# Requeueing three ScalarE operations in the first key groups: one exponential behind the next group's first fork copy, one behind its copy s7, one V copy behind the copy of a fifth product

## The chip, the cores and the metric

The kernel runs on one core of one Trainium2 chip. The metric is the device time of an execution in microseconds (us); 0.1% of it is 0.72 us. Engines: PE is TensorE, DVE is VectorE, ACT is ScalarE, POOL is GpSimd.

## The reference, cut to what matters

```python
x = A_x                                             # [1, 2048, 1024] bf16
q, k, v = split(layernorm(x) @ wqkv)                # 32 heads of 32
phi = lambda t: where(t > 0, t + 1, exp(t)) + 1e-6
kv = einsum("bhsd,bhse->bhde", phi(k), v)           # sums over all tokens
...                                                 # attention output, then a gated MLP
```

Only the beginning matters here: the layer norm, the k and v projections and the running sum `kv`.

## The kernel before

Tokens come in 16 tiles of 128. V of tiles 0 to 3 is computed by plain products ("V pieces"). Everything else is computed for pairs of tiles in groups of seven products instead of eight (a Strassen-like scheme on sums of input blocks). `k0` is the k projection of tiles 0 and 1, both halves of its columns; `v2` is V of tiles 4 and 5, and so on. Groups run in the order k0, v2, k1, v3, k2, v4. A PSUM bank is the buffer in which the matmuls of one product are summed. `hook(i)` runs what was left in `pend[i]` before, mostly by the previous group, then what the main part registered for that place. One group is:

```python
def sgroup(...):
    prod(a, X(0, 0), W(0, 0), True, "P1")                 # four matmuls into PSUM bank a
    ident_act(bank(b), bank(a), ..., name + "fk1")        # first fork: ACT copies bank a to bank b
    hook(1)
    prod(f, SX(2), TW(2), True, "P7")
    ident_act(s7, bank(f), ...)                           # copy s7
    hook(2)
    prod(b, SX(1), TW(1), False, "P6")                    # needs the first fork
    ident_act(bank(c), bank(b), ..., name + "fk2")        # second fork
    hook(3)
    prod(a, X(1, 0), W(1, 0), False, "P2")
    for f_ in e11(bank(a), B_bank[a]): f_()               # k group: exp on ACT, two DVE ops (phi)
    hook(4)
    prod(c, SX(0), TW(0), False, "P5")                    # needs the second fork
    ident_act(sc, bank(c), ...)                           # copy sc
    s22 = e22(bank(f), ..., sc, bc); s22[0]()             # DVE addition
    hook(5)
    prod(b, X(1, 1), TW(3), False, "P4")
    s21 = e21(bank(b), ..., s7, b7); s21[0]()             # DVE addition
    hook(6)                                               # v2: 64 small matmuls, the KV sum of tiles 0 and 1
    for f_ in s22[1:2]: f_()                              # exp of s22, on ACT
    prod(c, SX(3), W(1, 1), False, "P3")                  # overwrites what sc reads: waits for sc
    s12 = list(e12(bank(c), B_bank[c]))
    if isphi: s12.pop(0)()                                # exp of s12, on ACT
    ...
    pend[1] = list(s22[2:]) + s12 + list(s21[1:])         # run at hook(1) of the next group
    hook(7)
```

`SX` and `TW` are sums and differences of input and weight blocks, which DVE makes; I call them all sums. A phi step is the pair of DVE operations on lines 854 and 857 that follows an exponential. TensorE runs the products in this order; counted so, P7 is the second, P6 the third, P5 the fifth and P3 the last. Each engine takes its own operations in the order in which they are recorded.

Of the kernel before, what the change touches and what calls it, by code (L numbers as in the profile page):

```python
# [132 lines left out]
def bass_sequential_preLN__linear_attn_block__glu_gated_reglu__prompt_kernel(  # L133
# [71 lines left out]
    with es:  # L205
# [148 lines left out]
        def bank(b, w=512):  # L354
            return ps[:, b, 0:w]
# [184 lines left out]
        def alloc_bank(pool, copied=False):  # L540

            b = min((b for b in pool if not (copied and b in partial)), key=lambda b: bank_last[b])
            if not copied:
                partial.discard(b)
            touch_bank(b)
            return b
# [219 lines left out]
        def mm(out_ap, lhsT, rhs, start, stop, reads, bbuf, name, skip=False):  # L766
            return PL.add(
                "pe",
                lambda e: e.matmul(out_ap, lhsT, rhs, start=start, stop=stop, skip_group_check=skip),  # L769
                reads=reads, writes=[bbuf], name=name,  # L770
            )

        def ident_act(dst, src, reads, writes, name, func=ACTF.Identity):
            PL.add("act", lambda e: e.activation(out=dst, in_=src, func=func), reads=reads, writes=writes, name=name)  # L774
# [70 lines left out]
        def phi_steps(src, src_buf, dst_ap, dst_buf, name):  # L845
            k = phi_ctr[0] % NPH
            phi_ctr[0] += 1

            def ex():
                PL.add("act", lambda e: e.activation(out=Et[:, k, :], in_=src, func=ACTF.Exp),  # L850
                       reads=[src_buf], writes=[B_E[k]], name=name + "_exp")

            def fin():
                PL.add("dve", lambda e: e.tensor_scalar(out=Et[:, k, :], in0=Et[:, k, :], scalar1=1.0,  # L854
                                                      scalar2=1e-6, op0=ALU.min, op1=ALU.add),
                       reads=[], writes=[B_E[k]], name=name + "_e2")
                PL.add("dve", lambda e: e.scalar_tensor_tensor(out=dst_ap, in0=src, scalar=C1, in1=Et[:, k, :],  # L857
                                                               op0=ALU.add, op1=ALU.max),
                       reads=[src_buf, B_E[k]], writes=[dst_buf], name=name + "_phi")
            return ex, fin  # L860
# [84 lines left out]
        def xnT_buf(st, dc):  # L945
            return B_xnT[st][0 if dc < HDC else 1]
# [3 lines left out]
                b = banks[i % len(banks)]  # L950
                mm(bank(b, 512), zeros_t[:, 0:P], zeros_t, True, True, [B_zeros], B_bank[b], "dummy")

        def v_piece(st, h, mid=()):
            b = alloc_bank(P1_POOL)
            nt = ND2 + h
            mid = dict(mid)
            for dc in range(NDC):
                if dc in mid:
                    mid[dc]()
                if st < 2:  # L960
                    xa, bx = xcT[:, st, dc, :], B_xcT[st][dc // HDC]
                else:
                    xa, bx = xnT[:, dc, st * P:(st + 1) * P], xnT_buf(st, dc)
                mm(bank(b, NW), xa, wkv[:, dc, nt * NW:(nt + 1) * NW],
                   dc == 0, dc == NDC - 1, [bx, B_wkv[nt][0 if dc < WKH else 1]], B_bank[b],
                   "v_%d_%d" % (st, h))
            v_copy(b, st, h)

        v_k = {}

        def v_out(st, j):
            n0 = (st % NV) * H + j * GPN * HPG
            return vh[:, n0:n0 + GPN * HPG, 0:Dh]

        def gw(ap):
            return ap.rearrange("p (n w) -> p n w", w=Dh)

        def v_copy(b, st, j):
            sc, rd = (1.0, []) if st >= 2 else (rstd[:, v_k[st], :], [B_rstd[v_k[st]]])
            PL.add("act", lambda e: e.activation(out=v_out(st, j), in_=gw(bank(b)), func=ACTF.Identity, scale=sc),  # L980
                   reads=[B_bank[b]] + rd, writes=[B_v[st % NV][j]], name="v_%d_%d" % (st, j))
# [42 lines left out]
            add(1, s(0), xb(0, 0), ALU.subtract, [B_Sx[0][p]] + bx(0, 0))  # L1024
            add(3, xb(1, 0), s(1), ALU.subtract, [B_Sx[1][p]] + bx(1, 0))

        def sgroup(pool, tok_major, X, SX, W, TW, e11, e12, e21, e22, name, hooks=(), isphi=True, last=False):

            hooks = dict(hooks)

            def prod(b, x, w, start, nm):
                (xf, xr), (wf, wr) = x, w
                for kk in range(KH):
                    xa, wa = xf(kk), wf(kk)
                    l, r = (xa, wa) if tok_major else (wa, xa)
                    o = bank(b)
                    if len(r.shape) == 3:
                        o = o.rearrange("p (a b) -> p a b", b=r.shape[2])
                    mm(o, l, r, start and kk == 0, kk == KH - 1, xr + wr, B_bank[b], name + nm, skip=True)

            def hook(i):
                for f_ in pend.pop(i, ()):
                    f_()
                if i in hooks:
                    hooks[i]()

            a = alloc_bank(pool)
            f = alloc_bank(pool)
            b = alloc_bank(pool, True)
            prod(a, X(0, 0), W(0, 0), True, "P1")  # L1050
            ident_act(bank(b), bank(a), [B_bank[a]], [B_bank[b]], name + "fk1")
            hook(1)
            prod(f, SX(2), TW(2), True, "P7")
            grp[0] += 1
            s7, b7 = [(atmp, B_at), (btmp[:, 1, :], B_bt[1])][grp[0] % 2]
            sc, bc = btmp[:, 0, :], B_bt[0]
            ident_act(s7, bank(f), [B_bank[f]], [b7], name + "s7")
            hook(2)
            c = alloc_bank(pool, True)
            prod(b, SX(1), TW(1), False, "P6")  # L1060
            ident_act(bank(c), bank(b), [B_bank[b]], [B_bank[c]], name + "fk2")
            hook(3)
            prod(a, X(1, 0), W(1, 0), False, "P2")
            for f_ in e11(bank(a), B_bank[a]):
                f_()
            hook(4)
            prod(c, SX(0), TW(0), False, "P5")
            ident_act(sc, bank(c), [B_bank[c]], [bc], name + "sc")
            s22 = e22(bank(f), B_bank[f], sc, bc)
            s22[0]()  # L1070
            hook(5)
            prod(b, X(1, 1), TW(3), False, "P4")
            s21 = e21(bank(b), B_bank[b], s7, b7)
            s21[0]()
            hook(6)
            for f_ in s22[1:2]:
                f_()
            prod(c, SX(3), W(1, 1), False, "P3")
            s12 = list(e12(bank(c), B_bank[c]))
            if isphi:  # L1080
                s12.pop(0)()
            if last:
                pend[1] = s12 + [s21[1]]
                return [s22[2], s21[2]]
            pend[1] = list(s22[2:]) + s12 + list(s21[1:])
            hook(7)

        pend = {}
# [8 lines left out]
        def add_phi(dst, dst_buf, name):  # L1097
            def go(p_, pb, s_, sb_):
                def add():
                    PL.add("dve", lambda e: e.tensor_tensor(out=s_, in0=p_, in1=s_, op=ALU.add), reads=[pb],  # L1100
                           writes=[sb_], name=name + "_add")
                return (add,) + phi_steps(s_, sb_, dst, dst_buf, name)
            return go

        def x_ops(p):
            def X(k, t):
                st = 2 * p + t
                return (lambda kk: xnT[:, k * KH + kk, st * P:(st + 1) * P]), [B_xnT[st][k]]

            def SX(i):  # L1110
                return (lambda kk: Sx(i)[:, kk, p * P:(p + 1) * P]), [B_Sx[i][p]]
            return X, SX
# [26 lines left out]
        def k_group(p, hooks=()):  # L1139
            X, SX = x_ops(p)  # L1140
            W, TW = w_ops(wkv, bw_k, tw_k, B_TWk)

            def dst(t, h):
                st = 2 * p + t
                return pk_ap(st)[:, h * NW:(h + 1) * NW], B_pk[pk_slot(st)][h]

            def pl(t, h):
                d, db = dst(t, h)
                return lambda b, bb: phi_steps(b, bb, d, db, "k_%d_%d" % (2 * p + t, h))
            sgroup(P1_POOL, True, X, SX, W, TW, pl(0, 0), pl(0, 1),  # L1150
                   add_phi(*dst(1, 0), "k_%d_0" % (2 * p + 1)),
                   add_phi(*dst(1, 1), "k_%d_1" % (2 * p + 1)), "k%d" % p, hooks)

        def v_group(p, hooks=()):
            X, SX = x_ops(p)
# [844 lines left out]
        twk.pop(0)()  # L2000
        twv.pop(0)()
        twv.pop(0)()
        v_piece(3, 1)
        for i in range(2):
            load_wq(i)
        NP_ = NST // 2
# [50 lines left out]
        for p in range(NP_):  # L2057
            nq = NQ.get(p, (0, 0))
            hooks, sq = kv_hooks(p, nq)
# [5 lines left out]
            if p + 2 < NP_:  # L2065
                late = []
# [37 lines left out]
        for r in range(2):  # L2104
            for ct in range(NG // 2):
                hooks = {}
# [41 lines left out]
        for p_ in range(NPASS):  # L2148
            fill = []
            for q in range(NPAIR):  # L2150
# [5 lines left out]
                mid = [[], [], [], [], []]  # L2156
# [59 lines left out]
            late = []  # L2216
            if p_ + 1 < NPASS:
                late = [(lambda t=t: early_c(t), (0, t)) for t in range(STB)]
# [81 lines left out]
```

## Time and profile before

| | before |
|---|---|
| time, median of the first 3 runs | 722.19 us (722.02 to 722.98) |
| span of the profile | 720.5 us |
| PE, DVE, ACT busy | 99%, 82%, 50% |
| PE idle in 24 to 36 us | 1.07 us |

The prediction shows the rows of the profile. Two more lines of its timeline (start and duration in us, engine, line, operation) serve as marks from here on: the DVE sum after which DVE never rests until its last phi step in v2, and the first product of k1.

```profile
24.39 1.22 DVE L991 TENSOR_TENSOR RC<-RAB,RC 128x2048 f16<-128x2048 bf16 x1
36.88 1.03 PE L769 MATMUL ps<-RAB 128*128 128x512 bf16 x4
```

I call the start of that sum T. Here T is 24.39, and the first product of k1 starts at T + 12.49.

### The profile page before, as it was taken

How to read it: one execution, taken by the hardware profiler on the slowest of the kernel's cores; microseconds unless marked ns; L12 is line 12 of the kernel's file. 1: busy time of each engine (PE TensorE's matmuls, PEld its weight loads, DVE VectorE, ACT ScalarE, POOL GpSimd, SP SyncE). 2: the span in 40 equal slices, each digit the busy share in tenths (PEclk: the TensorE clock that was granted, in tenths of full speed). 3: DMA queues.
4: the chain of work that ended last, by engine and by line, in shares of the span. 5: the costliest groups of instructions: out<-in, count | busy, mean ns of one | idle time of the engine just before them, and what ended most of it. 6: DMA issues, size and time to landing. Idle time of an engine off the chain costs nothing.

```text
span 720.5 us, 12877 instructions
## 1 busy us (share of the span) xinstructions
PE 714.3 (99%) x4901; PEld 380.0 (53%) x4901; DVE 588.9 (82%) x1030; ACT 358.9 (50%) x626; POOL 110.8 (15%) x178
## 2 busy tenths in 40 slices
PE   8999999999999999999999999999999999999998
PEld 3344444444444444444444568865555555447887
DVE  6988867899776889888988787887889877888885
ACT  4977666764842466677756111035455445423010
POOL 3321100000350103332321001310000000000331
PEclk9999999999999999999999999999999999999999
DMA  9852344015998797999998999994554572037997
GB/s 295 260 113 65 38 136 157 9 30 97 216 202 264 222 284 236 276 320 297 296 281 266 313 251 317 318 215 119 145 169 139 160 245 84 1 95 248 322 323 183
DMA packets 195101, 144.17 MB, mean 200 GB/s; under 512 B 53984, under 2 KB 172512, under 8 KB 195040
## 3 DMA queue, kind: packets, MB, share of 16 engines
q1 hardware_dynamic: 190048, 138.77, 65.9%
q0 software_dynamic: 4032, 3.67, 3.6%
q10 hardware_dynamic: 960, 0.92, 0.4%
q8 instruction: 38, 0.62, 0.4%
q14 instruction: 23, 0.19, 0.1%
HBM read 98.76 MB, written 32.51 MB: 182 GB/s over the span
## 4 chain that ended last, share of the span: by engine, by line
PE 95%; DVE 2%; DMA 1%; ACT 1%; issue 1%; SPq 0%; ACTq 0%
PE ps L769 95%; DMA RAB<-in_A_wqkv_dram 1%; DVE RWG L1016 0%; DVE RE L857 0%; DVE RX L1100 0%; DVE RE L1674 0%; DVE RX L854 0%; DVE RH L1016 0%; ACT RXH L809 0%; DVE RC L991 0%; DVE RW L991 0%; ACT ps L774 0%; PE ps L910 0%; DVE RWG L1614 0%; SPq L567 0%
## 5 line engine op out<-in xcount | busy, mean ns | idle before, releaser
L774 ACT ACTIVATE ps<-ps 128x512 f32<-128x512 f32 (+1 forms) x193 | 108.9, 565 | 220.8 <-PE ps L769 212.1
L769 PE MATMUL ps<-RC,RO 128*128 128x512 f16 x616 | 143.0, 369 | 0.0
L769 PE MATMUL ps<-RH,RWG 128*128 128x512 bf16 x448 | 108.1, 379 | 0.0
L769 PEld LDWEIGHTS ps<-RC,RO 128*128 128x128 f16 x616 | 60.3, 98 | 63.5
L769 PE MATMUL ps<-RC,RWG 128*128 128x512 f16 x320 | 76.9, 379 | 0.3 <-ACT ps L774 0.2
L769 PEld LDWEIGHTS ps<-RH,RWG 128*128 128x128 bf16 x448 | 43.8, 98 | 46.9
L1483 DVE TENSOR_TENSOR RAB<-ps,RAB 128x512 bf16<-128x512 f32 x56 | 37.3, 686 | 31.3 <-PE ps L769 31.3
L769 PE MATMUL ps<-RH,RO 128*128 128x512 bf16 (+1 forms) x256 | 61.2, 379 | 0.0
L1683 POOL DMA_DIRECT2D out_dram<-RX x20 | 17.9, 1281 | 263.7 <-DVE RX L1674 221.5
L769 PE MATMUL ps<-RW,RE 128*128 128x512 bf16 x256 | 57.6, 380 | 0.0
L769 PE MATMUL ps<-RW,RAB 128*128 128x256 f16 (+3 forms) x362 | 52.9, 301 | 0.0
L769 PEld LDWEIGHTS ps<-RC,RWG 128*128 128x128 bf16 (+1 forms) x320 | 30.0, 98 | 40.3 <-ACT ps L774 6.3
L774 ACT ACTIVATE RE<-ps 128x512 f32<-128x512 f32 (+1 forms) x64 | 31.5, 503 | 37.8 <-PE ps L769 37.8
L769 PE MATMUL ps<-RAB 128*128 128x512 bf16 (+2 forms) x238 | 49.8, 348 | 0.0
L769 PEld LDWEIGHTS ps<-RW,RAB 128*128 128x128 f16 (+1 forms) x362 | 35.3, 98 | 14.5
L1674 DVE TENSOR_TENSOR RE<-ps,RE 128x512 f32<-128x512 f32 x44 | 30.2, 686 | 14.2 <-PE ps L769 13.7
L774 ACT ACTIVATE RAB<-ps 128x512 bf16<-128x512 f32 x56 | 33.3, 595 | 16.7 <-PE ps L769 16.4
L1367 DVE TENSOR_TENSOR RO<-RWG 128x1024 f16<-128x1024 bf16 x54 | 36.9, 684 | 4.5 <-DMA RWG<-in_B_W_up_dram 4.5
L769 PEld LDWEIGHTS ps<-RH,RO 128*128 128x128 f16 (+1 forms) x256 | 24.4, 98 | 29.9 <-ACT RX L774 1.5
L1478 ACT ACTIVATE RAB<-RAB 128x1024 bf16<-128x1024 bf16 x28 | 29.5, 1055 | 19.3 <-DVE RAB L1469 18.7
L1469 DVE TENSOR_TENSOR RAB<-ps,RE 128x512 bf16<-128x512 f32 x56 | 37.1, 685 | 2.1 <-PE ps L769 1.7
L769 PEld LDWEIGHTS ps<-RW,RE 128*128 128x128 bf16 x256 | 24.0, 98 | 27.9 <-DVE RXH L1265 0.4
(170 smaller groups left out, 1170.3 us busy)
## 6 DMA issues: line engine op xcount, KB each, us to landing
RWG<-in_B_W_gate_dram SPq DMA_DIRECT2D x28, 512.0 KB, 6.2
RWG<-in_B_W_up_dram SPq DMA_DIRECT2D x28, 512.0 KB, 5.2
RW<-l_scr SPq DMA_DIRECT2D x20, 448.0 KB, 5.6
RW<-in_B_W_down_dram SPq DMA_DIRECT2D x14, 512.0 KB, 5.4
t_scr<-RW SPq DMA_DIRECT2D x14, 512.0 KB, 4.8
l_scr<-RX SPq DMA_DIRECT2D x7, 1024.0 KB, 6.1
RE<-l_scr SPq DMA_DIRECT2D x15, 448.0 KB, 4.9
RE<-in_A_x_dram SPq DMA_DIRECT2D x23, 256.0 KB, 3.7
```

What stands on the lines that cost most here:

```text
L769: lambda e: e.matmul(out_ap, lhsT, rhs, start=start, stop=stop, skip_group_check=skip),
L774: PL.add("act", lambda e: e.activation(out=dst, in_=src, func=func), reads=reads, writes=writes, name=name)
L1367: PL.add(eng, lambda e: e.tensor_tensor(out=tb(j, u), in0=f0(u), in1=f1(u), op=ALU.subtract), reads=[B_w[i + x] for x in r] + ([B_T[k + x] ...
L1469: PL.add("dve", lambda e: e.tensor_tensor(out=d, in0=src, in1=ftmp[:, u, :], op=ALU.add), reads=[bsrc, B_s5[u]], writes=[db], name=name)
L1478: PL.add("act", lambda e: e.activation(out=d, in_=d, func=ACTF.Relu), reads=[], writes=db, name=name)
L1483: PL.add("dve", lambda e: e.tensor_tensor(out=d, in0=bank(b), in1=d, op=ALU.mult), reads=[B_bank[b]], writes=[db], name=name)
L1674: PL.add(eng, lambda e: e.tensor_tensor(out=dst, in0=in0, in1=in1, op=op), reads=reads, writes=writes, name=name)
L1683: PL.add("pool", lambda e: e.dma_start(dst, src, accum_op=ALU.add), reads=[bsrc], writes=[B_hscr[st]], slot=sl, name="acc_%d_%d" % (st, dh))
```

## The change

The intent is to let the fork copies, on which TensorE waits, run earlier on ACT, by queueing operations behind them that nobody needs soon.

```diff
-        def v_piece(st, h, mid=()):
+        def v_piece(st, h, mid=(), late=False):
 ...
-            v_copy(b, st, h)
+            if late:
+                pend[5] = [lambda: v_copy(b, st, h)]      # behind sc of the next group, k0
+            else:
+                v_copy(b, st, h)
 ... in sgroup:
-            if isphi:
+            if isphi and not lazy:
                 s12.pop(0)()
 ...
-            pend[1] = list(s22[2:]) + s12 + list(s21[1:])
+            if lazy:
+                pend[1] = s12[:1] + list(s22[2:]) + s12[1:]   # exp of s12 behind the first fork
+                pend[2] = list(s21[1:])                       # exp of s21 behind s7
+            else:
+                pend[1] = list(s22[2:]) + s12 + list(s21[1:])
 ... in k_group: lazy=p < 2          # k0 and k1, so the forks of v2 and v3
 ... in the main part:
-        v_piece(3, 1)
+        v_piece(3, 1, late=True)
```

Only the ACT queue changes its order; the other four queues are the same.

More of the change, by code (lines that the diff above doesn't have):

```diff
@@ L1025, in x_sums, with sgroup @@
             add(3, xb(1, 0), s(1), ALU.subtract, [B_Sx[1][p]] + bx(1, 0))
-        def sgroup(pool, tok_major, X, SX, W, TW, e11, e12, e21, e22, name, hooks=(), isphi=True, last=False):
+        def sgroup(pool, tok_major, X, SX, W, TW, e11, e12, e21, e22, name, hooks=(), isphi=True, last=False, lazy=False):
             hooks = dict(hooks)
@@ L1151, in k_group @@
                    add_phi(*dst(1, 0), "k_%d_0" % (2 * p + 1)),
-                   add_phi(*dst(1, 1), "k_%d_1" % (2 * p + 1)), "k%d" % p, hooks)
+                   add_phi(*dst(1, 1), "k_%d_1" % (2 * p + 1)), "k%d" % p, hooks, lazy=p < 2)
         def v_group(p, hooks=()):
```

## The prediction

> **What bounds the kernel now.** First the page: its busy row, to see which engine is full.
>
> ```profile
> PE 714.3 (99%) x4901; PEld 380.0 (53%) x4901; DVE 588.9 (82%) x1030; ACT 358.9 (50%) x626; POOL 110.8 (15%) x178
> ```
>
> TensorE (PE) is busy in 714.3 us of a span of 720.5 us, and the clock row of the page shows it at 0.9 or more in every slice. Nothing that only reorders ScalarE (ACT) can therefore gain more than the few microseconds in which PE stands still. The change touches the stretch from the end of the direct V pieces to the second V group, some 23 to 50 us, so I took busy time by stretch next (columns: stretch, its length, then PE, weight load, DVE, ACT, POOL busy).
>
> ```profile
> 24.00:36.00 12.00, 10.93 (x110) 4.47 (x109) 11.76 (x20) 10.78 (x24) 3.11 (x7) 1.00 0.81 254
> 36.00:45.00 9.00, 8.94 (x52) 3.58 (x40) 8.52 (x21) 6.80 (x16) 2.82 (x7) 1.00 0.54 119
> 45.00:51.00 6.00, 5.96 (x89) 2.84 (x90) 5.66 (x13) 4.34 (x9) 0.00 (x0) 1.00 0.27 53
> ```
>
> In 24 to 36 us PE is idle for 12.00 - 10.93 = 1.07 us; in the next two stretches for 0.06 and 0.04 us. So what can be won lies in the first stretch, and there VectorE (DVE) is fuller than PE: 11.76 of 12.00 us. Third, the timeline of that stretch, PE alone (start, duration):
>
> ```profile
> 23.31 1.03 PE L769 MATMUL ps<-RC,RWG 128*128 128x512 f16 x4
> 24.54 1.04 PE L769 MATMUL ps<-RC,RWG 128*128 128x512 f16 x4 [0.20 <-ACT ps L774]
> ...
> 29.73 1.03 PE L769 MATMUL ps<-RW,RWG 128*128 128x512 f16 x4
> 31.56 1.04 PE L769 MATMUL ps<-RW,RWG 128*128 128x512 f16 x4 [0.81 <-ACT ps L774]
> ```
>
> These are products of four matmuls. In a run without waits they start 0.865 us apart (27.14, 28.00, 28.86, 29.73). From 23.31 to 24.54 is 1.23 us, so 0.36 us is lost at the first fork copy of group k0; from 29.73 to 31.56 is 1.83 us, so 0.96 us is lost at that of v2. Both wait for the fork copy on ACT (line 774, the tile ps to ps), and these are the waits that the change aims at.
>
> Last, what stands after them, from the same timeline for DVE and PE:
>
> ```profile
> 34.02 0.69 DVE L857 SCALAR_TENSOR_TENSOR RE<-ps,RX 128x512 bf16<-128x512 f32 x1
> 34.62 0.28 DVE L854 TENSOR_SCALAR RX<-RX 128x512 bf16<-128x512 bf16 x1
> 34.94 0.69 DVE L857 SCALAR_TENSOR_TENSOR RE<-RX 128x512 bf16<-128x512 f32 x1
> 35.24 0.83 PE L769 MATMUL ps<-RE 128*32 128x33 bf16 x64
> 36.00 1.04 PE L769 MATMUL ps<-RAB,RH 128*128 128x512 bf16 x4
> ```
>
> The 64 small matmuls add tokens 0 and 1 to the KV sum. The quarter for tile 1's first half needs the DVE operation that runs from 34.94 to 35.63; the chain of waits shows PE starting again at 35.69, and 32 matmuls later, at 36.00, the last product of v2 follows. So PE already waits there for DVE. How long has DVE been late? In the timeline its only idle time is 0.46 us before 23.93, for a rstd from POOL. From 23.93 to 35.63 every start follows the one before at the pitch the operation has elsewhere (1.14 us for a 128x2048 sum, 0.60 for an addition, 0.32 then 0.61 for the two halves of phi). **DVE, not ACT, sets the time at which PE leaves this stretch.**
>
> **What the Trainium skill says.** "PSUM — Partial Sum Buffer", section Engine vs sequencer instructions: the queues of ScalarE and VectorE are strict FIFO. That is the whole lever of this change (a fork copy ready early still waits behind what is queued ahead), and the trace agrees: the copy at 30.91 follows two exponentials at 29.90 and 30.44 though its product began at 28.86. "ScalarE: Activation LUTs", section What ACT_TABLE_LOAD costs: an activation runs at one element per cycle for every function, and back-to-back ones overlap by about 93 ns. The trace agrees roughly: exponential and copy take 0.58 to 0.63 us and start 0.47 to 0.54 us apart, so swapping them costs nothing by itself. "Perfetto Trace Analysis", section Tensor Engine Instruction: the end of a matmul in the profile is an estimate. I therefore reckon with starts only. No page bears on how long an ACT wait for PE takes; I take it from the trace.
>
> **The change part by part.** Nothing is added or removed. Comparing the programs' order, PE, DVE, POOL and SP are identical; only ACT has three moves.
>
> Two measures first. Where ACT sits idle, a fork copy starts 1.12 to 1.13 us after its product starts (36.88 to 38.00; 56.28 to 57.41), and PE's next product starts 0.63 to 0.66 us after the copy starts (38.00 to 38.63; 30.91 to 31.56).
>
> 1. V copy of tile 3 (0.58 us at 23.41), moved behind the copy "sc" of k0. k0's first product began about 23.31 - 0.87 = 22.44, so the fork can start at 22.44 + 1.13 = 23.57 instead of 23.89 and the next product at 24.22 instead of 24.54: 0.32 us earlier. Some is lost again inside k0: the second fork is ready at 25.35, the fifth product at 26.00, sc at 27.13, and the last product waits for sc (27.13 + 0.66 = 27.79). v2 then begins at 28.65 instead of 28.86: 0.21 us earlier. The V copy now runs at about 27.6, then the 1.05 us statistic, ending near 29.25. ACT has idled 0.93 us before 29.90 for a DVE addition, so both fit and the exponential at 29.90 stays.
>
> 2. v2: the fork goes before one exponential. It cannot pass the exponential at 29.90, which was queued earlier, so it starts at about 30.42 instead of 30.91, and the third product at 31.07 instead of 31.56 (0.49 us). The exponentials then follow at 30.92 and 31.88; the second fork is at 32.41 instead of 32.77, the fifth product at 33.06 instead of 33.41. PE would reach the small matmuls at about 34.89 instead of 35.24, **0.35 us earlier, and stop at the quarter that DVE delivers at 35.63.** DVE's order is unchanged and all its inputs come before it needs them (exponentials ending about 31.5 and 32.5 for operations at 33.70 and 34.62). So PE resumes at 35.69 as before: 0.00 us gained.
>
> 3. v3: at 43.05 its first product starts; the fork is ready at 44.18 and ran at 44.39. Now it runs at 44.18 and the third product starts at 44.83 instead of 45.04. But the queue up to the second fork holds the same five activations, and the fork now makes ACT idle from 43.92 to 44.18: copies and exponentials at 44.68, 45.15, 45.64, second fork at 46.16 instead of 46.11. The fifth product starts at 46.16 + 0.65 = 46.81 instead of 46.77. So 0.21 us is won and given back two products later: 0.04 us lost.
>
> Sum: 0.00 + 0.04 us on 722.19 us, that is, no change that a timing can see: 722.2 us.
>
> **The rivals.**
>
> The chain of waits is right and ACT is the bound. It shows the V copy and the fork as pieces of the path:
>
> ```profile
> 23.50 0.49 ACT RE L980
> 23.99 0.50 ACT ps L774
> ...
> 27.34 0.61 ACT RX L774
> 27.94 0.28 DVE RX L854
> ```
>
> If the steps from ACT to DVE are real, part 1 brings DVE forward. Against it: the DVE operation at 27.92 comes 1.14 us after the sum at 26.78, its ordinary pitch, and its input (the exponential at 26.71) was done at 27.30; the view attributes the step to the last signal. If I am wrong here, the gain is up to the 1.07 us of idle PE time in 24 to 36 us: 721.1 us.
>
> A new wait. The late V copy holds its PSUM bank some 4 us longer; the program shows v2's first fork copy now writes into that bank and waits for ACT itself as well as PE. By the above the copy ends near 28.2, before the fork at 30.4. Also, should the statistic for tile 7 slip, its normalisation at 38.20 could. It has a second of two halves running after 34.37 anyway, so the slip is not on that path. If one of these did bind: 0.3 to 0.6 us lost, 722.5 to 722.8 us.
>
> DVE itself shifts. POOL gates DVE at 23.93 and takes its numbers from ACT at 20.82 to 22.0, before the first move. So no gain and no loss from there.
>
> **Range and chances.** I give about 75% to no visible change, 17% to a gain of 0.3 to 1.1 us and 8% to a loss of that kind. Three runs of the kernel before lie between 722.02 and 722.98, so a median may move by half a microsecond by itself. Range: 721.3 to 723.0 us. A change of 2% would be 14 us, thirteen times the idle time of PE in the stretch that the change can reach: faster 0.4%, same 99.2%, slower 0.4%.
>
> **What would show it.** Right, if the idle time before the third products of k0 and v2 falls (0.20 to about 0, 0.81 to about 0.5), if a wait of PE for DVE line 857 appears or grows to about 0.4 us just before 35.69, if v2's last product still starts at 36.00 and DVE is without idle time from 23.93 to 35.63; and if in v3 the fifth product starts within 0.1 us of 46.77. Wrong, if v2's last product starts clearly before 35.9, which would mean that DVE did follow ACT; or if DVE shows idle time there, waiting for an exponential that moved.

## The result, and the profile after

| | before | after |
|---|---|---|
| median | 722.35 us (722.02 to 722.98, 4 runs) | 722.80 us (722.38 to 723.14, 4 runs) |
| span of the profile | 720.5 us | 720.8 us |
| T | 24.39 | 24.72 |
| first product of k1 | T + 12.49 | T + 12.48 |

The ratio is 1.0005, 95% interval 0.9988 to 1.0022: the same. (The ratio is not the ratio of the medians, which is 1.0006 here.)

The queue of ACT at the first fork of v2, before and then after: two exponentials stood ahead of the fork copy, now one does.

```profile
29.90 0.63 ACT L850 ACTIVATE RX<-RX 128x512 bf16<-128x512 f32 x1 [0.93 <-DVE RX L1100]
30.44 0.58 ACT L850 ACTIVATE RX<-ps 128x512 bf16<-128x512 f32 x1
30.91 0.59 ACT L774 ACTIVATE ps<-ps 128x512 f32<-128x512 f32 x1
```

```profile
30.23 0.63 ACT L850 ACTIVATE RX<-RX 128x512 bf16<-128x512 f32 x1 [0.83 <-DVE RX L1107]
30.76 0.58 ACT L774 ACTIVATE ps<-ps 128x512 f32<-128x512 f32 x1
31.28 0.58 ACT L850 ACTIVATE RX<-ps 128x512 bf16<-128x512 f32 x1
```

The timeline after: two DVE lines, the mark T and the last phi step of v2, then the PE lines from the second product of k0 on.

```profile
24.72 1.22 DVE L994 TENSOR_TENSOR RC<-RAB,RC 128x2048 f16<-128x2048 bf16 x1
35.27 0.69 DVE L857 SCALAR_TENSOR_TENSOR RE<-RX 128x512 bf16<-128x512 f32 x1
```

```profile
23.20 1.03 PE L769 MATMUL ps<-RC,RWG 128*128 128x512 f16 x4
24.49 1.02 PE L769 MATMUL ps<-RC,RWG 128*128 128x512 f16 x4 [0.26 <-DVE RC L994]
...
31.40 1.04 PE L769 MATMUL ps<-RW,RWG 128*128 128x512 f16 x4 [0.71 <-ACT ps L774]
...
33.40 1.04 PE L769 MATMUL ps<-RW,RWG 128*128 128x512 f16 x4
34.27 1.03 PE L769 MATMUL ps<-RW,RAB 128*128 128x512 f16 x4
35.23 0.38 PE L769 MATMUL ps<-RE 128*32 128x33 bf16 x32
36.02 0.38 PE L769 MATMUL ps<-RE 128*32 128x33 bf16 x32 [0.40 <-DVE RE L857]
...
37.20 1.03 PE L769 MATMUL ps<-RAB 128*128 128x512 bf16 x4
```

Read them against T, not against the clock, because T itself moved by 0.33 us. The third product of v2 started at T + 7.17 before (31.56) and at T + 6.68 after: 0.49 us earlier. The small matmuls began at T + 10.85 and now at T + 10.51: 0.34 us earlier. Then the second half of them waits for DVE, and it starts at T + 11.30 in both kernels (35.69 and 36.02). DVE's last phi step starts at T + 10.55 in both (34.94 and 35.27). The gain has become the wait of 0.40 us on line 857, and k1 starts at the same T + 12.48 or 12.49. In the kernel before, DVE was the last by little: from the start of the small matmuls to k1 it is 1.64 us there, 1.97 us after, and 1.51 us in `dve_minus` below, where nothing waits. So DVE cost PE 0.13 us before and 0.46 us after.

### The profile page after: what moved, and what is told of

The parts are those of the page before. It is cut to its first block, busy times and chain, and to the rows that moved or that the text cites. A ratio compares the mean times of both kernels' runs of the same rounds, so it can differ in the third digit from the quotient of the medians.

```text
span 720.8 us, 12822 instructions
## 1 busy us (share of the span) xinstructions
PE 710.7 (99%) x4846; PEld 380.4 (53%) x4901; DVE 588.9 (82%) x1030; ACT 358.8 (50%) x626; POOL 110.0 (15%) x178
## 4 chain that ended last, share of the span: by engine, by line
PE 94%; DMA 2%; DVE 1%; issue 1%; ACT 1%; SPq 0%; ACTq 0%
PE ps L769 94%; DMA RE<-in_A_x_dram 1%; DMA RAB<-in_A_wqkv_dram 1%; SPq L567 0%; ACT ps L774 0%; DVE RC L994 0%; ACT RX L850 0%; DVE RE L857 0%; DVE RE L1681 0%; DVE st L783 0%; DVE RW L994 0%; ACT RXH L774 0%; DVE RWG L1621 0%; ACT RXH L809 0%; DVE RX L854 0%
## 5 line engine op out<-in xcount | busy, mean ns | idle before, releaser
L769 PE MATMUL ps<-RH,RO 128*128 128x512 bf16 (+1 forms) x228 | 55.2, 379 | 1.5
```

Source lines behind the costliest of these rows:

```text
L769: lambda e: e.matmul(out_ap, lhsT, rhs, start=start, stop=stop, skip_group_check=skip),
```

## The experiments

All experiments were read by T, because a whole execution varies by more than the change can do. "k1" is the start of k1's first product. The last phi step of v2 starts at T + 10.55 or 10.56 in the first six rows.

| run | T | k1 after T | span | span - T |
|---|---|---|---|---|
| before | 24.39 | 12.49 | 720.5 | 696.1 |
| before_again | 25.00 | 12.49 | 721.1 | 696.1 |
| after | 24.72 | 12.48 | 720.8 | 696.1 |
| after_again | 24.50 | 12.49 | 720.6 | 696.1 |
| v_only | 24.27 | 12.49 | 720.4 | 696.1 |
| lazy_only | 24.44 | 12.48 | 720.5 | 696.1 |
| act_plus | 24.44 | 12.69 | 720.7 | 696.3 |
| dve_plus | 25.07 | 15.00 | 723.6 | 698.5 |
| dve_minus | 24.97 | 12.02 | 720.5 | 695.5 |
| kv_late_before | 24.69 | 12.11 | 720.8 | 696.1 |
| kv_late_after | 24.64 | 11.78 | 720.4 | 695.8 |
| best | 24.26 | 11.10 | 721.0 | 696.7 |
| best2 | 24.21 | 11.12 | 720.1 | 695.9 |

In the last four rows the small matmuls that stood in front of k1, half or all of them, come behind its first product, so the third column is not comparable there and the last one is.

**The same two programs again.** No edit.

> The changed kernel once more, unaltered. Theory (VectorE sets when TensorE leaves v2): ratio to the kernel before within 0.9990 to 1.0010, no sign settled. In its trace the gap between the start of v2's seventh product and its third-listed product stays near 1.73 us (1.83 in the kernel before), and the last product of v2 starts 0.3 to 0.4 us after the end of the last phi step on VectorE, wherever that lies. If VectorE's chain starts as early as in the kernel before (its 128x2048 sum at 24.39 rather than 24.72), the product starts near 36.0 again. Rival (the change itself makes VectorE late by 0.33 us): the chain starts at about 24.7 again, and in no trace of the kernel before.

> The kernel before against itself: what a ratio shows where nothing differs. Ratio 0.9990 to 1.0010. Its trace is the second one of this program: if the start of VectorE's chain moves between 24.3 and 24.8 us without any change of the program, the 0.33 us by which the changed kernel's profile is later is no effect of the change; if it lies at 24.39 again, that reading loses ground.

Measured: after_again 722.31 us, ratio 1.0002 (0.9988 to 1.0015); before_again, the kernel before against itself, 722.60 us, ratio 1.0003 (0.9991 to 1.0016). Nothing separates the change from no change. In after_again the v2 pitch was 1.66 us (expected near 1.73), the rest as expected. The trace of before_again settles where the 0.33 us came from; its DVE lines:

```profile
21.81 1.23 DVE L991 TENSOR_TENSOR RC<-RAB 128x2048 f16<-128x2048 bf16 x1 [1.04 <-DMA RAB<-in_A_wqkv_dram]
...
25.00 1.22 DVE L991 TENSOR_TENSOR RC<-RAB,RC 128x2048 f16<-128x2048 bf16 x1
```

An unchanged program had T at 25.00, later than the changed one, after DVE had waited 1.04 us for a load of key weights. The same wait (1.13 us) stands in the profile after, and not in the first profile before. So a later T needs no change of the program, and T accounts for the whole difference between the two profiled spans: span less T is 696.1 us in all six rows.

**One part at a time.** `v_only` has `lazy=False`; `lazy_only` has the V copy in its old place.

> Only the V copy is moved; the exponentials stay. Theory: the fork of k0 starts directly behind the 1.05 us statistic, so that the idle time of TensorE before k0's second product that needs it falls from 0.36 us in pitch to under 0.1 us, unless VectorE's sum for that product is late, as in the changed kernel's profile; the fork of v2 still runs behind two exponentials, and the pitch there stays at 1.8 to 1.9 us. The last product of v2 follows the end of VectorE's last phi step by 0.3 to 0.4 us. Rival (chain of waits right): that product comes 0.2 to 0.35 us earlier than in the kernel before with VectorE's chain starting at the same time.

> Only the exponentials are moved; the V copy stays. Theory: in k0 the pitch of 1.23 us stays (the fork behind the V copy); in v2 the pitch falls from 1.83 to 1.3 to 1.75 us, and the time won ends in a wait for VectorE's last phi step of 0.2 to 0.5 us; in v3 the third product comes 0.2 to 0.3 us earlier after the group's start and the fifth within 0.05 us of before (3.72 us after the group's start). The last product of v2 follows the end of VectorE's last phi step by 0.3 to 0.4 us. Rival: the last product of v2 comes about 0.4 us earlier relative to the start of VectorE's chain.

Measured: in `v_only` the loss at k0's fork is gone (second product at 23.19, fourth at 24.92: 1.73 us, two free pitches), the pitch at v2's fork grew to 2.2 us, more than the 1.8 to 1.9 expected because PE arrived earlier at the same fork, and the time is 722.13 us for one run. In `lazy_only` the small matmuls began early and waited 0.40 us for DVE; 722.25 us for one run. Two pitches there missed the forecast: 1.39 us at k0's fork (1.23 expected), and about 1.2 us at v2's (1.3 to 1.75 expected; reckoned back from the fourth product at 32.00, because the view joins the second and the third). Each part does its work on ACT's queue, and in both k1 starts at T + 12.48 or 12.49. The rival, a step from ACT to DVE, would have shown there as 0.2 to 0.4 us less.

In `lazy_only` v3 also behaves as in the changed kernel. PE lines of v3, first, fourth and fifth product, in the kernel before and then in the changed kernel (in `lazy_only` the distances are 2.60 and 3.70 us):

```profile
43.05 1.03 PE L769 MATMUL ps<-RAB 128*128 128x512 bf16 x4
...
45.91 1.03 PE L769 MATMUL ps<-RAB 128*128 128x512 bf16 x4
46.77 1.03 PE L769 MATMUL ps<-RW,RWG 128*128 128x512 f16 x4
```

```profile
43.38 1.03 PE L769 MATMUL ps<-RAB 128*128 128x512 bf16 x4
...
45.97 1.03 PE L769 MATMUL ps<-RAB 128*128 128x512 bf16 x4
47.08 1.04 PE L769 MATMUL ps<-RW,RWG 128*128 128x512 f16 x4
```

From the first product to the fourth it is 2.86 us before and 2.59 after, so the third came 0.27 us earlier; to the fifth it is 3.72 and 3.70. The second fork ends the same queue of five activations either way: from the first of them to the second fork it is 2.71 us before (43.40 to 46.11) and 2.69 after (43.72 to 46.41). What changed is where ACT stands still, ahead of the second fork before and ahead of the first one after. So the gain is given back one wait later.

**More DVE work, more ACT work.** The first edit does one weight sum three times; the second does the exponential of s22 in k0 twice. Both on top of the change, results unchanged.

```diff
         twv.pop(0)()
         twv.pop(0)()
+        again()            # the last of these sums once more
+        again()            # and once more
         v_piece(3, 1, late=True)
```

```diff
-            for f_ in s22[1:2]:
+            for f_ in s22[1:2] * (2 if name == "k0" else 1):
                 f_()
```

> The changed kernel with one VectorE sum of 128x2048 (1.22 us, 1.14 to 1.25 us of pitch) done three times instead of once, results unchanged: 2.3 to 2.5 us more VectorE work ahead of v2. Theory (VectorE is what TensorE follows out of v2): TensorE leaves v2 2.3 to 2.5 us later counted from the start of the VectorE chain, that is, the first product of k1 starts 14.8 to 15.0 us after the sum that starts at 24.72 in the changed kernel, instead of 12.48, and the whole execution is about 2.4 us longer: ratio to the kernel before 1.0020 to 1.0045. Rival (ScalarE is the bound and VectorE has slack in this stretch): under 0.5 us, ratio under 1.0015.

> The changed kernel with one ScalarE exponential ahead of v2's fork done twice (0.53 us more, the result the same). Theory: the fork and the third product of v2 slip by about 0.53 us against the start of the VectorE chain, the wait for VectorE's last phi step shrinks from 0.40 us to nothing, and k1's first product slips by only 0.00 to 0.15 us (12.48 to 12.63 us after the chain's start). Rival (ScalarE is the bound): k1's first product slips by 0.45 to 0.55 us.

Measured with more DVE work: k1 at T + 15.00, that is 2.52 us later, one for one with DVE's last phi step (T + 13.07 instead of 10.55), and span less T 2.4 us longer. The timing is 725.32 us, ratio 1.005 (1.0037 to 1.0064), above the 1.0045 expected. Four of its five runs show a granted clock of 0.995 to 0.998, all nine of the kernel before in those rounds 1.0, so part of the excess may be the clock; that was not shown. The profiled run had T at 25.07, 0.68 us later than in the first profile before, which together with the 2.4 us gives its span of 723.6; whether T is later in all runs of this kernel was not measured. PE lines, the second product of v2, the wait for the last phi step and the first product of k1:

```profile
32.52 1.04 PE L769 MATMUL ps<-RW,RWG 128*128 128x512 f16 x4 [2.34 <-DVE RWG L1019]
...
38.88 0.38 PE L769 MATMUL ps<-RE 128*32 128x33 bf16 x32 [0.41 <-DVE RE L857]
...
40.07 1.03 PE L769 MATMUL ps<-RAB 128*128 128x512 bf16 x4
```

The last wait is no longer than without the extra work (0.41 and 0.40 us): the delay enters earlier, at v2's second product, which waits 2.34 us for a DVE sum. ACT slips with it, because the exponential ahead of the fork waits for a DVE addition that comes later too. So this run shows that PE hangs on DVE's chain as a whole; that it is the last phi step and not ACT behind that addition is shown by the next run and by `dve_minus`.

Measured with more ACT work: the repeated exponential cost 0.67 us at the fork, not 0.53 (the two executions take 1.29 us against 0.63 for one, so they did not overlap), so the small matmuls began at T + 11.18 instead of T + 10.51. They then ran in one piece without a wait:

```profile
35.62 0.71 PE L769 MATMUL ps<-RE 128*32 128x33 bf16 x64
...
37.13 1.03 PE L769 MATMUL ps<-RAB 128*128 128x512 bf16 x4
```

Of 0.67 us only 0.21 came out (k1 at T + 12.69); 0.46 us was swallowed by the wait for DVE. I had expected up to 0.15. The rival said 0.45 to 0.55.

**Less DVE work.** The fourth weight sum of V is left out and a raw block read in its place (relative error 0.41). Its output is wrong, which doesn't matter for the time.

```diff
-            return TWv[:, j]
+            return TWv[:, j] if j < 3 else wkv[:, KH:2 * KH, D:D + NW]
...
-                    twv.pop(0)()
+                    twv.pop(0)
```

> The changed kernel with one VectorE sum less (the fourth weight sum of V, 1.22 us at 31.96, left out; the fourth product of the V groups reads a raw weight block in its place, so V and the output are wrong on purpose; every matmul stays in size and place). Theory: VectorE's last phi step comes 1.13 us earlier and is no longer what TensorE waits for, so the 64 small matmuls run in one piece; the first product of k1 starts 11.9 to 12.15 us after the start of the VectorE chain instead of 12.48, and the span less the start of that chain falls from 696.1 to 695.5 to 695.8. Not the whole 1.13 us, since ScalarE's forks and the products themselves hold v2 next. Rival (VectorE was no bound): 12.4 to 12.5 us and 696.1.

Measured: the wait on line 857 is gone, k1 starts at T + 12.02 and span less T is 695.5 us, both as expected. The sum left out stands behind the DVE addition that ACT waits for, so ACT's fork stays at T + 6.05 (6.04 in the changed kernel) and only the phi steps come earlier. Of 1.13 us taken from DVE, 0.46 us reaches PE. Then ACT's fork holds it, for which the third product of v2 still waits 0.70 us until T + 6.68, and the products behind it:

```profile
35.48 0.71 PE L769 MATMUL ps<-RE 128*32 128x33 bf16 x64
...
36.99 1.03 PE L769 MATMUL ps<-RAB 128*128 128x512 bf16 x4
```

**The wait for DVE taken away from both kernels.** Tile 1's half of the KV sum is moved from v2 behind the first product of k1. The result is correct.

```diff
 def v6(p=p, nq=nq):
-    kvaccs(p)
+    if p == 0:
+        kvacc(0)
+    else:
+        kvaccs(p)
 ...
+if p == 1:
+    hooks[1] = lambda k1_=hooks[1]: (kvacc(1), k1_())
```

> The kernel before, with tile 1's half of the KV accumulation taken out of v2 and put behind the first product of k1, so that v2 no longer waits for VectorE's last phi step. Results unchanged. Theory: the last product of v2 then waits for the ScalarE copy sc of v2 (start plus 0.66 us), which comes at the same place of the ScalarE queue as ever, so little is won: the seventh product of k1, the second of the group, starts 13.25 to 13.40 us after the VectorE sum that starts at 24.39 in the kernel before (there 13.35). Time: ratio 0.9988 to 1.0010.

> The changed kernel with the same move of tile 1's half of the KV accumulation. Theory: with the wait for VectorE out of the way, the 0.35 us that the change wins on ScalarE reach the end of v2: the second product of k1 starts 12.90 to 13.10 us after the start of the VectorE chain (13.35 in both kernels now), 0.25 to 0.45 us earlier than in the kernel before with the same move, and it stays won to the end of the execution. Ratio to the kernel before 0.9980 to 1.0005. Rival (the change wins nothing on ScalarE's own path): the same 13.25 to 13.40 us as the kernel before with the move.

Measured ("the second product of k1" is P7 of the source): T + 13.38 on the kernel before and T + 13.05 on the changed kernel. With DVE's wait out of the way the change is worth 0.33 us, and it stays: span less T is 696.1 and 695.8. On the kernel before the move alone wins nothing: it saves the 0.13 us that DVE cost there, but the last product of v2 then waits some 0.08 us for the copy sc, and the small matmuls in two blocks take some 0.07 us more than in one. PE lines of the kernel before with the move, the last product of v2 and the second of k1; then the same two of the changed kernel with the move:

```profile
36.16 0.81 PE L769 MATMUL ps<-RAB,RH 128*128 128x512 bf16 x3 [0.23 <-ACT RX L774]
...
38.07 1.90 PE L769 MATMUL ps<-RC,RWG 128*128 128x512 f16 x8
```

```profile
35.77 0.81 PE L769 MATMUL ps<-RAB,RH 128*128 128x512 bf16 x3 [0.23 <-ACT RX L774]
...
37.69 1.90 PE L769 MATMUL ps<-RC,RWG 128*128 128x512 f16 x8
```

(The "x3" is a product whose first record is missing from the trace, so it started one matmul of 0.216 us earlier, at 35.94 and 35.55, and most of the 0.23 us shown is that gap.) Both starts lie 0.66 us behind the start of sc (35.28 and 34.89), which is how they show the wait for it; a block of 32 small matmuls that nothing holds up lets the next product start after 0.31 us, which would be 35.86 and 35.47, so 0.08 us is waited. Timed, they are 722.14 us (ratio 1.0002, 0.9989 to 1.0014) and 722.16 us (1.0004, 0.9990 to 1.0017): 0.33 us of 722 is 0.05%, and these runs do not resolve it. Only the trace shows it.

**Two attempts at more.** Both put all of the first two KV sums behind the next group's first product, the fork of v2 and v3 ahead of all three exponentials, and the statistics of tile 8 (1.7 us of DVE) later.

```diff
-            for f_ in s22[1:2]:
+            for f_ in (() if lazy else s22[1:2]):
                 f_()
...
-                pend[1] = s12[:1] + list(s22[2:]) + s12[1:]
-                pend[2] = list(s21[1:])
+                pend[1] = [s22[1], s12[0], s22[2], s12[1]]
+                pend[3] = list(s21[1:])
... v6: kvaccs(p) only for p > 1; k groups 1 and 2, hook 1: kvaccs(p - 1)
... v4, v5 of p = 0: second half statistic of tile 7 behind sc
... best:  statistics of tile 8 in v3 at hook 3, its normalisation at hook 5
... best2: statistics of tile 8 at hook 7 of k1, its normalisation in its old place
```

> An attempt at a version ahead of both: the changed kernel with both tiles' KV accumulations of the first two pairs behind the next group's first product, the fork of v2 and v3 ahead of all three exponentials, the third of them behind the second fork, the second half statistic of tile 7 behind the copy sc, and VectorE's statistics of tile 8 (1.7 us) behind the phi steps of k1. Results unchanged. Theory: neither ScalarE's forks nor VectorE's last phi step hold TensorE out of v2; the first product of k1 starts 10.7 to 11.3 us after the start of the VectorE chain (12.48 now), k1's second product 11.9 to 12.6 us (13.35 now), and the span less the start of the chain falls from 696.1 by 0.5 to 1.3 us. In time that is at most 0.2 per cent, near what five rounds can tell: ratio 0.9970 to 1.0000.

> The same attempt with its fault mended: the statistics of tile 8 now stand at the end of k1 on VectorE, ahead of that group's phi steps, and the normalisation of tile 8 is back in its old place, so that its transposing transfer starts at most about 1.5 us later than in the changed kernel. Theory: the first products of k1 and v3 come as early as in the first attempt (11.10 and 18.06 us after the start of the VectorE chain, 12.48 and 18.66 in both kernels compared), the first product of v4 no longer waits for a transfer or for less than 0.3 us, and the span less the start of the chain is 695.2 to 695.8 us instead of 696.1. Ratio 0.9975 to 1.0005. Rival: the transfer for tile 8 still comes late, and the difference is given back as in the first attempt (696.1 or more).

Measured: in `best` k1 and its second product come at T + 11.10 and T + 12.77 (a little later than the 11.9 to 12.6 expected for the latter), but the later normalisation delays the transfer (a DMA) that writes the normalised tile 8 transposed for the products, and v4 then waits for it; span less T is 696.7, 0.6 us worse, and the time 722.72 us (ratio 1.0009, 0.9995 to 1.0022). The PE line:

```profile
56.61 1.02 PE L769 MATMUL ps<-RAB 128*128 128x512 bf16 x4 [0.55 <-DMA RAB<-RXH]
```

`best2` has no such wait. v3 starts 0.58 us earlier (T + 18.08 instead of 18.66), but its last product waits 0.22 us for the copy sc and v4 starts only 0.23 us earlier (T + 31.66 instead of 31.89). Span less T is 695.9 against the 695.2 to 695.8 expected, the time 722.50 us, ratio 0.9997 (0.9985 to 1.0010). By their traces, one each, the smaller edit kv_late_after (695.8) and best2 (695.9) are level within the rounding of the span, and none is faster by the clock.

## Why the prediction was right, point by point

- **DVE sets when PE leaves v2: right, and shown.** In the first six rows T varies by 0.73 us, ACT's order takes four forms, and k1 stays at T + 12.48 or 12.49. More ACT work came out to a third; less DVE work behind the addition that ACT waits for brought k1 forward by 0.46 us with ACT's fork in place. More DVE work came out one for one, but moves ACT too and settles less. The margin was thin: in the kernel before, DVE cost PE 0.13 us there, less than the 0.35 us that the change wins ahead of it. The timings alone do not separate this from a gain of 0.3 us; the traces do.
- **Part 1, the V copy.** The fork of k0 moved as said, but in the profile after the third product of k0 still waited, for DVE (0.26 us, line 994), because DVE's chain, and T with it, was late in that execution. In `v_only`, with an early T, the loss is gone. The forecast 0.21 us for the start of v2 was too small: from k0's second product to v2's first it is 5.55 us before and 5.18 in `v_only`, 0.37 us less. The loss forecast inside k0 did not come, because a copy starts 1.06 to 1.07 us after its product there, not 1.13. No effect at the end, as said. The late copy disturbed nothing: the tile 7 statistic ended before ACT had to wait for the DVE addition.
- **Part 2, v2.** The forecast 0.49 and 0.35 us for the third and the fifth product; against T they measure 0.49 and 0.34. The idle time before the third product fell only to 0.71 us, not to about 0.5. That term was mis-sized because I reckoned with one fixed T: PE's arrival and the fork's start do not move together, since the fork follows a DVE addition and so T. The wait for line 857 was forecast at 0.4 and is 0.40. (Where the prediction says tokens 0 and 1, it means tiles 0 and 1.)
- **Part 3, v3.** The third product won 0.27 us (forecast 0.21: the fork started 1.07 us after its product, not 1.13) and the fifth 0.02 us (forecast a loss of 0.04): given back, as said.
- **The rivals.** The chain of waits named the V copy, the fork and sc as pieces of the path; the one-part experiments show that no gain on ACT reaches DVE here. The bank held longer cost nothing. My upper bound for the first rival, 1.07 us, was too wide: without the DVE wait the change is worth 0.33 us.
- **What the prediction did not see.** A second wait stands right behind the first: v2's last product also waits for the copy sc, some 0.08 us once DVE is out of the way. And the variation of half a microsecond between executions has a place, T.

Open: which load makes T early or late, and why. In the six profiles with T at 24.64 or later DVE had waited 0.85 to 1.29 us for a load of key weights; in the seven with T at 24.50 or earlier it waited instead for a rstd (the reciprocal standard deviation of the layer norm) from POOL, just ahead of T. No run varied that.

## What to carry to other kernels

Before moving a copy forward for an engine that waits on it, follow that engine to its next wait and ask whether the other side of that one moves too; here it was an engine busy 11.76 of 12.00 us. Compare small changes from a mark inside the trace (here a DVE operation after which DVE never rests), not from the start of the execution. And a gain can end at the next wait if the queue up to it holds the same work in total, as at v3's second fork.

## What the Trainium skill lacked or had wrong

- "TensorE: Matmul & The Clock Gate", section Back-to-back issue gap, gives about 131 ns for each matmul of 512 columns as the sustained pace of LDWEIGHTS and MATMUL pairs, and calls its isolated formula (about 216 ns) an over-count there. In this kernel, at a granted clock of 1.00, four such pairs take 0.865 us wherever nothing waits, which is 216 ns each: the isolated figure is the pace.
- "VectorE: DVE Perf Modes", section The DRAIN you can't avoid, says that a semaphore after each operation costs nothing extra. A 128x2048 sum that waits for the sum directly ahead of it starts 1.25 us after it, an independent one 1.14 us after (26.78 and 25.53 us in the kernel before): 0.11 us for the dependence. The page's test does not say whether its operations waited on one another.
- "ScalarE: Activation LUTs", section What ACT_TABLE_LOAD costs, gives an overlap of about 93 ns of activations back to back; the trace agrees (0.58 us long, 0.47 to 0.48 us apart). It has no figure for an activation that waits for the one directly ahead: the repeated exponential cost 0.67 us instead of the 0.53 us of its ordinary pitch.
- No page has the time from a product to a copy of it and on to the next product: here 1.06 to 1.13 us from the start of four matmuls to the start of the ACT copy, and 0.63 to 0.67 us from there to the start of the product that needs it.
